# A fused attention and gated MLP block on one Trainium2 core: four tiles of x transposed once instead of twice, and the second half's preparation put on a fixed timetable

## The chip, the core and the metric

The kernel runs on one core of a Trainium2 chip. The metric is the device time of one execution in microseconds (us). The engines are TensorE (PE in the profile, with its weight loads as PEld), VectorE (DVE), ScalarE (ACT), GpSimd (POOL) and SyncE (SP), which here issues most of the DMAs. Each engine works through a queue of its own in order, and semaphores hold an instruction until its operands are there.

## The reference

```python
def reference(A_x, A_k_cache, A_v_cache, A_wq, A_wo, B_x, B_w_in, B_w_sp, B_b_sp, B_w_out):
    def _A_ref(x, k_cache, v_cache, wq, wo):      # 32 heads of 128, keys: the last 512
        q = (x @ wq).reshape(B, Sq, Hq, Dh).transpose(0, 2, 1, 3)
        k, v = k_cache[:, :, Sk - W:, :], v_cache[:, :, Sk - W:, :]
        scores = jnp.einsum("bhqd,bhkd->bhqk", q, k) * (Dh ** -0.5)
        o = jnp.einsum("bhqk,bhkd->bhqd", _softmax(scores), v)
        return o.transpose(0, 2, 1, 3).reshape(B, Sq, Hq * Dh) @ wo
    def _B_ref(x, w_in, w_sp, b_sp, w_out):
        z = _gelu(x @ w_in)
        z1, z2 = z[..., :Fh], _layernorm(z[..., Fh:])
        g = jnp.einsum("ts,bsf->btf", w_sp, z2) + b_sp[None, :, None]
        return (z1 * g) @ w_out
    xn = _layernorm(A_x)
    return A_x + _A_ref(xn, ...) * _silu(_B_ref(xn, ...))
```

x is 2048 rows of 512; Fh is 688. All is float32.

## The kernel before

Every float32 product is made of three TensorE matmuls: each operand is split into a high part (a rounded copy, made by ACT) and a low part (the rest, a subtraction on DVE or POOL), and `mm3` adds high by high, low by high and high by low. x is cut into 16 tiles of 128 rows, T8 = 8 in each half.

**The opening.** Tiles 0 to 7 are loaded into `sacc`, normalized (`ln_open` takes the statistics, `ln_apply` and `ln_apply_late` apply them) and transposed. `ln_flip(i)` makes four 128 by 128 transpositions against the unit matrix `ident` into one PSUM bank, ACT copies the high halves into the blocks `X`, and DVE subtracts for the low halves (`rest`). Tiles 4 to 7 have besides a copy of half the bank to `sacc` (L237) and one subtraction (L244), since q's projection is made with seven block products in place of eight (Strassen's scheme, Winograd's form): it needs sums T1 to T4 of quarters of x. Those pair tile p with tile p + 4. `t_sums(p)` transposes tile p a second time (line L215) and makes the sums in three subtractions and additions of 256 columns (L250 to L252); `t_split(p)` splits them. Between the transpositions stand pieces of z = x w_in (`z1_piece`, 12 matmuls of 344 columns), stored to DRAM by ACT's own DMA queue.

**The attention loop.** A step t makes for one tile of queries of one head the scores (`score`, lines L65 to L67 on `qT`), the maximum (`nm`, DVE's reduction at L530), the exponentials (ACT, L532), and for earlier steps the transposition of the probabilities (`turn`, DVE, L541, through DRAM: `p_dram`), their split (`shares`: ACT L560, POOL `pT_l`), the product with V (`pv`, L568 to L570), and the product with w_o (`outp`, L65 to L67 on `oT`), which DVE adds to `sacc` (L592). Four steps are a block; 16 steps are a round g of q's projection (`q_products`, L503, with `q_sum`, `q_split`, `q_evict`, `q_done`). I call s = (t + 12) mod 16 the phase of a step in its round. In a step, what the table `todo` holds comes before the score's reduction in DVE's, ACT's and POOL's order; the list `late` comes at the step's end, after `turn`.

**The second half of x.** The tiles 8 to 15 are prepared during the loop, in four passes p = 0 to 3 of `later_x(p)`, 48 steps (three rounds) apart. A pass loads two tiles (a and b), takes statistics (`tile_stats`), turns the variance into a factor (`row_stats`, with the small DVE operation at L74), applies it (ACT), transposes through DVE and DRAM (`turn_x`, `send`, `fetch`, `ordered`), and makes the quarter sums on POOL (`part`, and `sums(0)` to `sums(3)` at L356), which are stored to DRAM. Before, the rows of this sequence stood at t = max(t + 2, 30 + 12n // 5), every two or three steps: the statistics of a pass at t = 37 and 39, `row_stats` at 42, the two turns at 46 and 49, `part` at 63, the sums at 66, 68, 70 and 73 (for p = 0).

PSUM has eight banks in two pools of four. `ps_acc` holds q's products, `pv` and most z tiles, `ps_step` the scores, `outp` and, in the opening, the transpositions; both hand out their banks in turn. After the loop z's second half is made, tile by tile, each read by ACT's gelu (L846); the pools are then given up and the products with w_sp begin (L932) in the same banks.

Of the kernel before, what the change touches and what calls it, by code (L numbers as in the profile page):

```python
# [8 lines left out]
F32 = mybir.dt.float32  # L9
# [3 lines left out]
OP = mybir.AluOpType  # L13
# [27 lines left out]
def mixer_kernel(ctx: ExitStack, tc: tile.TileContext, x, wh, w_in, w_sp, b_sp, w_out, out):  # L41
# [8 lines left out]
    nc = tc.nc  # L50
# [10 lines left out]
    late = []  # L61
# [21 lines left out]
    ps_acc = psum.enter_context(tc.tile_pool(name="ps_acc", bufs=4, space=PSUM))  # L83
    ps_step = psum.enter_context(tc.tile_pool(name="ps_step", bufs=4, space=PSUM))
# [127 lines left out]
    def flip(t, late=False):  # L212
        ps = ps_acc.tile([P, NC, P], F32, name="ps_a") if late else ps_step.tile([P, NC, P], F32, name="ps_3")
        for c in range(NC):
            nc.tensor.transpose(ps[:, c, :], t[:, c * P:(c + 1) * P], ident)  # L215
        return ps

    def ln_flip(i, parts=1):
        n, j = divmod(i, 4)
        if j == 0:  # L220
            for h in range(2):
                X[0][h, n] = block()
        if parts == 1:
            ps = flip(sacc[:, i, :])
        else:
            ps = ps_step.tile([P, NC, P], F32, name="ps_3")
        rests, rest_of = [], []
        for h in range(2):
            if parts > 1:
                for c in (2 * h, 2 * h + 1):  # L230
                    nc.tensor.transpose(ps[:, c, :], sacc[:, i, c * P:(c + 1) * P], ident)
            hi, lo = (quarter(X[0][h, n][:, a], j) for a in range(2))
            nc.scalar.copy(hi, ps[:, 2 * h:2 * h + 2])
            rests.append((lo, ps[:, 2 * h:2 * h + 2], hi))
        if n == 1:
            p2, y = ps.rearrange("p c q -> p (c q)"), sacc[:, i, :]
            nc.scalar.copy(y[:, :256], p2[:, :256])  # L237
            rest_of.append((y[:, 256:], p2[:, 256:], y[:, :256]))
        if parts > 1:
            return rests  # L240
        for r in rests:
            rest(nc.vector, *r)
        for r in rest_of:
            nc.vector.tensor_tensor(*r, op=OP.subtract)  # L244

    TS = ("T2", "T1", "T3", "T4")

    def row_sums(ps, y, o):

        nc.vector.tensor_tensor(o[:, :256], y[:, :256], ps[:, :256], op=OP.subtract)  # L250
        nc.vector.tensor_tensor(o[:, 256:], ps[:, :256], y[:, 256:], op=OP.add)
        nc.vector.tensor_tensor(y[:, :256], ps[:, 256:], o[:, 256:], op=OP.subtract)  # L252

    def t_sums(p):
        if p == 0:
            X[0].update((k, block()) for k in TS)
        row_sums(flip(sacc[:, p, :]).rearrange("p c q -> p (c q)"), sacc[:, 4 + p, :], sacc[:, p, :])

    def t_split(p):
        y, o = sacc[:, 4 + p, :], sacc[:, p, :]  # L260
# [38 lines left out]
    def later_x(p):  # L299

        a, b, key = T8 + p, T8 + 4 + p, 100 * (p + 1)
        t, nb = {}, {}

        def row():
            return xq.tile([P, 512], F32, name="rawx")
# [52 lines left out]
        def store(*ks):  # L358
            for k in ks:
# [7 lines left out]
                                      t[k].bitcast(F32).rearrange("p (a c q) -> p a c q", a=2, q=P))  # L367

        seq = [load, None, None, lambda: tile_stats(t[a], key, 0), lambda: tile_stats(t[b], key, 1), row_stats,
               lambda: apply(b),  # L370
               lambda: (turn_x(b), apply(a)),
               lambda: turn_x(a),
               None,
               lambda: fetch(b),
# [33 lines left out]
    def z1_out(i, n, ps):  # L408
        z = zs.tile([P, NB], F32, name="z1")
        nc.scalar.copy(z, ps[:, :NB])  # L410
        nc.scalar.dma_start(z1_dram[:, i, n * NB:(n + 1) * NB], z)

    def z1_piece(i, n, between=lambda: None):
        z1_out(i, n, z1_product(i, n, between))
# [182 lines left out]
    T0, T1 = -QL, NSTEP + OL  # L597
# [3 lines left out]
    def at(t, f, *args):  # L601
        todo.setdefault(t, []).append((f, args))
# [52 lines left out]
                q_events.setdefault(t0 + done + 2, []).append((q_done, g, k))  # L655

    for p in range(4):
        at(-3 + p, t_sums, p)
        at(-2 + p, t_split, p)
    ends = {}  # L660
    ends.setdefault(-2, []).append((keep_x, (0, 1)))
# [7 lines left out]
    ends.setdefault(16 * (NG - 1) - LEAD + 9, []).append((fetch_x, 1, (0, 1)))  # L669
    for k in ((0, 0), (1, 0)):  # L670
        ends.setdefault(NSTEP + 6, []).append((fetch_x, 0, k))
    n, t = 0, 28
    for p in range(4):
        seq, store = later_x(p)
        for k, (f, ks) in enumerate(seq):
            t = max(t + 2, 30 + 12 * n // 5)
            for key in ks:
                at(t, store, key)
            if f:
                at(t, f)  # L680
            n += 1

    load_x(0, 1)
    load_early(0, [(0, 2)])
# [9 lines left out]
    ident = const.tile([P, P], F32, name="ident")  # L694
# [22 lines left out]
    ps = ps_step.tile([P, 512], F32, name="ps_3")  # L717
# [8 lines left out]
    ps = ps_step.tile([P, 512], F32, name="ps_3")  # L726
# [6 lines left out]
    ps = ps_acc.tile([P, 512], F32, name="ps_a")  # L733
# [8 lines left out]
    rest(nc.vector, *lowq)  # L742
    z1_out(0, 1, ps)
    z1_out(1, 1, ps1)
    ln_apply(rows[4], 4)
    ln_apply(rows[5], 5)
    z1_piece(2, 0)
    ln_open(6)
    ln_open(7)
    z1_piece(2, 1)  # L750

    FILL = dict(zip((-7, -6, -5, -4, -3, -2, -1, 0, 1, 8),
                    [(i, 1) for i in range(3, T8)] + [(i, 0) for i in range(4, T8)] + [(3, 0)]))
# [2 lines left out]
    for t in range(T0, T1):  # L756
# [6 lines left out]
        i = t + XL  # L763
# [21 lines left out]
        if t in DRAIN:  # L785
            ps = z1_product(*DRAIN[t])
# [21 lines left out]
    ps = z1_product(*LAST[-1])  # L808
# [422 lines left out]
```

## Time and profile before

| what | value |
|---|---|
| device time, median of 3 runs | 1761.42 us (1761.37 to 1762.11) |
| the profiled execution, its own time | 1761.58 us |
| its span, first to last instruction | 1759.7 us |
| busy: PE, PEld, DVE | 1753.1, 1503.3, 1489.9 us |
| busy: POOL, ACT | 1239.4, 1185.8 us |
| granted TensorE clock | 1.0 of full speed throughout |

The profiled execution's span leaves out what lies before the first and after the last instruction, 1.9 us here. A busy share says how long an engine had an instruction in hand. Matmuls overlap in the pipeline: one of 512 columns lasts 0.39 us in the rows, but the next one starts some 0.23 us after it, so short waits of PE don't show as idle time; they show in the distances between starts.

### The profile page before, as it was taken

To read this page: it belongs to the slowest core of one execution; us is meant where nothing else is said; L and a number is where in the kernel's file an instruction comes from. 1 tells how busy PE (TensorE), PEld (TensorE's weight loads), DVE (VectorE), ACT (ScalarE), POOL (GpSimd) and SP (SyncE) were. 2 spreads that over 40 slices of the span, in tenths; PEclk is the share of its full clock that TensorE was granted. 3 is DMA by queue.
4 is the path that set the end of the run, shared out by engine and by line. 5 is a ranking of instruction groups with operands and counts; after the bars stand their busy time and mean duration, and the time that the engine had idled before them with its cause. 6 is when DMAs were issued, how large, how long until landed. Compare 5 with 4: busy or idle time off the path is not lost.

```text
span 1759.7 us, 28541 instructions
## 1 busy us (share of the span) xinstructions
PE 1753.1 (100%) x8431; PEld 1503.3 (85%) x8431; DVE 1489.9 (85%) x2458; ACT 1185.8 (67%) x2621; POOL 1239.4 (70%) x1171
## 2 busy tenths in 40 slices
PE   9999999999999999999999999999999999999999
PEld 8888888888888887888888888888888899999997
DVE  6789889899899889988888888888888647887875
ACT  5877777777777777777777777777777546543333
POOL 2888998988988989888888888888888411000032
PEclk9999999999999999999999999999999999999999
DMA  6688888988989989788787777877888652655496
GB/s 204 213 237 260 260 250 242 261 240 244 269 246 253 258 235 273 223 255 223 223 228 219 232 225 220 226 218 225 229 224 255 210 192 86 223 189 176 149 259 204
DMA packets 177468, 398.45 MB, mean 226 GB/s; under 512 B 24480, under 2 KB 58528, under 8 KB 158112
## 3 DMA queue, kind: packets, MB, share of 16 engines
q1 hardware_dynamic: 172704, 390.99, 75.7%
q10 hardware_dynamic: 4608, 5.64, 0.9%
q8 instruction: 66, 1.08, 0.3%
q14 instruction: 90, 0.74, 0.1%
HBM read 231.65 MB, written 164.89 MB: 225 GB/s over the span
## 4 chain that ended last, share of the span: by engine, by line
PE 99%; ACT 0%; DVE 0%; issue 0%; POOL 0%; DVEq 0%; POOLq 0%; ACTq 0%
PE ps_a L503 17%; PE ps L65 13%; PE ps L67 13%; PE ps L66 13%; PE ps L932 11%; PE ps_a L570 7%; PE ps_a L569 7%; PE ps_a L568 7%; PE ps_a L66 2%; PE ps_a L67 2%; PE ps_a L65 2%; PE ps_f L66 1%; PE ps_f L67 1%; PE ps_f L65 1%; PE ps_f L932 1%; PE ps_f L1139 0%
## 5 line engine op out<-in xcount | busy, mean ns | idle before, releaser
L59 POOL TENSOR_TENSOR pT_l<-pL,pT_h 128x512 fp32r<-128x512 f32 x507 | 659.2, 1303 | 170.9 <-ACT pT_h L560 162.6
L532 ACT ACTIVATE prob<-ps,nm 128x512 f32<-128x512 f32 x512 | 353.6, 691 | 340.8 <-DVE nm L530 331.8
L592 DVE SCALAR_TENSOR_TENSOR sacc<-ps,sums,sacc 128x512 f32<-128x512 f32 x496 | 369.3, 745 | 115.0 <-PE ps L67 109.4
L503 PE MATMUL ps_a<-x,x 128*128 128x512 f32 x1266 | 365.5, 389 | 0.0
L541 DVE STREAM_TRANSPOSE pL<-prob 128x512 f32<-128x512 f32 x512 | 358.6, 700 | 0.4 <-ACT prob L532 0.4
L530 DVE TENSOR_REDUCE nm<-ps 128x1 f32<-128x512 f32 x512 | 339.9, 664 | 3.0 <-PE ps L67 2.9
L560 ACT CAST pT_h<-pL 128x512 fp32r<-128x512 f32 x512 | 318.5, 622 | 7.3 <-ACT z L410 4.9
L503 PEld LDWEIGHTS ps_a<-x,x 128*128 128x128 f32 x1266 | 237.7, 188 | 49.3 <-issue 0.2
L59 POOL TENSOR_TENSOR wl<-raw,wh 128x512 fp32r<-128x512 f32 x186 | 241.9, 1300 | 11.0 <-ACT wh L145 11.0
L65 PE MATMUL ps<-wh,qT_h 128*128 128x512 f32 x512 | 200.7, 392 | 0.3 <-DVE sacc L592 0.2
L67 PE MATMUL ps<-wh,qT_l 128*128 128x512 f32 x512 | 200.0, 391 | 0.0
L570 PE MATMUL ps_a<-pT_l,wh 128*128 128x512 f32 x512 | 199.6, 390 | 0.0
L65 PE MATMUL ps<-wh,oT_h 128*128 128x512 f32 x512 | 199.4, 390 | 0.0
L66 PE MATMUL ps<-wl,qT_h 128*128 128x512 f32 x512 | 199.4, 389 | 0.0
L66 PE MATMUL ps<-wl,oT_h 128*128 128x512 f32 x512 | 199.4, 389 | 0.0
L568 PE MATMUL ps_a<-pT_h,wh 128*128 128x512 f32 x512 | 199.4, 389 | 0.0
L569 PE MATMUL ps_a<-pT_h,wl 128*128 128x512 f32 x512 | 199.4, 389 | 0.0
L67 PE MATMUL ps<-wh,oT_l 128*128 128x512 f32 x512 | 199.3, 389 | 0.0
L932 PE MATMUL ps<-b,x 128*128 128x344 f32 x1248 | 191.8, 316 | 0.0
L932 PEld LDWEIGHTS ps<-b,x 128*128 128x128 f32 x1248 | 191.5, 188 | 0.0
L59 POOL TENSOR_TENSOR b<-b 128x512 fp32r<-128x512 f32 x2 | 2.5, 1293 | 189.5 <-DMA x<-x 189.5
L59 POOL TENSOR_TENSOR x<-wq,x 128x256 fp32r<-128x256 f32 x177 | 131.6, 744 | 0.0
(212 smaller groups left out, 3047.7 us busy)
## 6 DMA issues: line engine op xcount, KB each, us to landing
p_dram<-pL SPq DMA_DIRECT2D x128, 1024.0 KB, 4.8
pL<-p_dram SPq DMA_DIRECT2D x256, 192.0 KB, 4.1
raw<-wh SPq DMA_DIRECT2D x188, 256.0 KB, 6.3
pL<-p_dram SPq DMA_DIRECT2D x256, 128.0 KB, 4.1
x<-w_sp SPq DMA_DIRECT2D x24, 1024.0 KB, 5.1
pL<-p_dram SPq DMA_DIRECT2D x256, 64.0 KB, 4.0
wq<-wh SPq DMA_DIRECT2D x60, 256.0 KB, 5.7
z_dram<-z ACTq DMA_DIRECT2D x32, 172.0 KB, 3.0
```

Source lines behind the costliest of these rows:

```text
L59: engine.tensor_tensor(lo, whole, hi.bitcast(F32), op=OP.subtract)
L65: nc.tensor.matmul(ps, lh, rh, start=first, stop=False)
L66: nc.tensor.matmul(ps, lh, rl, start=False, stop=False)
L67: nc.tensor.matmul(ps, ll, rh, start=False, stop=last)
L503: nc.tensor.matmul(qps[g, bank], wt["q", g, k][a][:, c * P:(c + 1) * P], X[g * 2 // H][ORDER[k]][:, b, c], start=first, stop=r == 5, skip_ ...
L530: nc.vector.tensor_reduce(nm, ps, axis=AX.X, op=OP.max, negate=True)
L532: nc.scalar.activation(prob[t], ps, AF.Exp, bias=nm, accum_out=sums[b][:, j:j + 1])
L541: nc.vector.transpose(pL[b][:, :, j * P:j * P + P].rearrange("p a (c q) -> p a c q", q=Q), prob.pop(t).rearrange("p (a c q) -> p a c q", a ...
L568: nc.tensor.matmul(pps[b], vh, ph, start=c == 0, stop=False)
L570: nc.tensor.matmul(pps[b], vh, pl, start=False, stop=c == 3)
L592: nc.vector.scalar_tensor_tensor(at, ps, rs, at, op0=OP.mult, op1=OP.add)
L932: nc.tensor.matmul(ps, a, b, start=k != "P4" and c == 0 and m == 0, stop=c == RP - 1 and m == 2, skip_group_check=True)
```

## The change

Three things change. First, tiles 0 to 3 are transposed once: ACT copies the whole bank of each transposition to SBUF (`keep_whole`, four copies of 128 by 512 between the z pieces of the opening; the first two transpositions go to `ps_acc` for that), and the sums are made from this copy at the end of the steps in which tiles 4 to 7 are transposed, in four subtractions (`row_sums`, after the other work of the step, in `late`). `t_sums` with its transpositions is gone; `t_blocks` only sets up the blocks. Second, one transposition of the unit matrix stands ahead of the last z tile, which moves that tile to the next bank. Third, the passes of `later_x` have a table of steps, 28 + 48 p plus 4, 14, 17 and so on, and the two applications stand together in one step.

```diff
+    def keep_whole(i):
+        p2, whole[i] = whole[i], xq.tile([P, 512], F32, name="rawx")
+        nc.scalar.copy(whole[i], p2)
...
         if parts == 1:
-            ps = flip(sacc[:, i, :])
+            ps = flip(sacc[:, i, :], i == 1)
         else:
-            ps = ps_step.tile([P, NC, P], F32, name="ps_3")
-        rests, rest_of = [], []
+            ps = ps_acc.tile([P, NC, P], F32, name="ps_a")
+        rests = []
...
+        p2 = ps.rearrange("p c q -> p (c q)")
         if n == 1:
-            p2, y = ps.rearrange("p c q -> p (c q)"), sacc[:, i, :]
+            y = sacc[:, i, :]
             nc.scalar.copy(y[:, :256], p2[:, :256])
-            rest_of.append((y[:, 256:], p2[:, 256:], y[:, :256]))
+            late.append((row_sums, p2, y, sacc[:, i - 4, :], whole[i - 4]))
+        whole[i] = p2
...
-    def row_sums(ps, y, o):
-
-        nc.vector.tensor_tensor(o[:, :256], y[:, :256], ps[:, :256], op=OP.subtract)
-        nc.vector.tensor_tensor(o[:, 256:], ps[:, :256], y[:, 256:], op=OP.add)
-        nc.vector.tensor_tensor(y[:, :256], ps[:, 256:], o[:, 256:], op=OP.subtract)
-
-    def t_sums(p):
-        if p == 0:
-            X[0].update((k, block()) for k in TS)
-        row_sums(flip(sacc[:, p, :]).rearrange("p c q -> p (c q)"), sacc[:, 4 + p, :], sacc[:, p, :])
+    def row_sums(ps, y, o, x):
+
+        for to, x0, x1 in ((y[:, 256:], ps[:, 256:], y[:, :256]), (o[:, :256], ps[:, :256], x[:, :256]),
+                           (o[:, 256:], ps[:, 256:], o[:, :256]), (y[:, :256], x[:, 256:], o[:, 256:])):
+            nc.vector.tensor_tensor(to, x0, x1, op=OP.subtract)
...
-               lambda: apply(b),
-               lambda: (turn_x(b), apply(a)),
+               lambda: (apply(b), apply(a)),
+               lambda: turn_x(b),
...
+    STORE_X = {"b": 32, "a": 33, (1, 1): 45, (0, 0): 46, (1, 0): 46, (0, 1): 48, "T1": 48, "T3": 49, "T2": 50, "T4": 51}
+    WHEN_X = (4, 0, 0, 14, 17, 18, 20, 30, 31, 0, 38, 39, 43, 44, 46, 47, 48, 49, 50)
...
-            t = max(t + 2, 30 + 12 * n // 5)
+            t = 28 + 48 * p + (WHEN_X[k] if k < len(WHEN_X) else 0)
...
+    keep_whole(0)
     ln_apply(rows[4], 4)
     ln_apply(rows[5], 5)
-    z1_piece(2, 0)
+    z1_piece(2, 0, lambda: keep_whole(1))
     ln_open(6)
     ln_open(7)
-    z1_piece(2, 1)
+    z1_piece(2, 1, lambda: (keep_whole(2), keep_whole(3)))
...
+            if (pos, n) == (NT - 1, 3):
+                nc.tensor.transpose(ps_acc.tile([P, 512], F32, name="ps_a")[:, :P], ident, ident)
```

Three places show what moves. On PE, at step -3 of the opening (the end of q's first projection, `x_185` by the query weights `wh_325`, and the start of the z piece of tile 7), before:

```order
L65 MATMUL ps_a<-x_185,wh_325 128x512
L66 MATMUL ps_a<-x_185,wh_325 128x512
L67 MATMUL ps_a<-x_185,wl_326 128x512
L215 MATMUL ps_542<-ident,sacc 128x128 x4
L65 MATMUL ps_a<-wh_245,x_405 128x344
L66 MATMUL ps_a<-wl_246,x_405 128x344
L67 MATMUL ps_a<-wh_245,x_405 128x344
```

and now, on the same engine at the same place:

```order
L65 MATMUL ps_a<-x_185,wh_325 128x512
L66 MATMUL ps_a<-x_185,wh_325 128x512
L67 MATMUL ps_a<-x_185,wl_326 128x512
L65 MATMUL ps_a<-wh_245,x_413 128x344
L66 MATMUL ps_a<-wl_246,x_413 128x344
L67 MATMUL ps_a<-wh_245,x_413 128x344
```

The row of four transpositions is gone; it goes likewise at steps -2, -1 and 0, and nothing else of PE's order changes but the one transposition ahead of the last z tile.

On DVE, at steps -7 and -6 of the opening (the low halves of tiles 4 and 5, and the application of the statistics to tiles 6 and 7), before:

```order
L59 TENSOR_TENSOR x_405<-ps_407,x_405 128x2x128
L59 TENSOR_TENSOR x_406<-ps_407,x_406 128x2x128
L244 TENSOR_TENSOR sacc<-ps_407,sacc 128x256
L200 SCALAR_TENSOR_TENSOR sacc<-sacc,mv,rs_r 128x512
L59 TENSOR_TENSOR x_405<-ps_439,x_405 128x2x128
L59 TENSOR_TENSOR x_406<-ps_439,x_406 128x2x128
L244 TENSOR_TENSOR sacc<-ps_439,sacc 128x256
L200 SCALAR_TENSOR_TENSOR sacc<-sacc,mv,rs_r 128x512
```

and now (`rawx` is ACT's copy of the earlier tile, in SBUF):

```order
L59 TENSOR_TENSOR x_413<-ps_415,x_413 128x2x128
L59 TENSOR_TENSOR x_414<-ps_415,x_414 128x2x128
L200 SCALAR_TENSOR_TENSOR sacc<-sacc,mv,rs_r 128x512
L258 TENSOR_TENSOR sacc<-ps_415,sacc 128x256
L258 TENSOR_TENSOR sacc<-ps_415,rawx 128x256
L258 TENSOR_TENSOR sacc<-ps_415,sacc 128x256
L258 TENSOR_TENSOR sacc<-rawx,sacc 128x256
L59 TENSOR_TENSOR x_413<-ps_450,x_413 128x2x128
L59 TENSOR_TENSOR x_414<-ps_450,x_414 128x2x128
L200 SCALAR_TENSOR_TENSOR sacc<-sacc,mv,rs_r 128x512
```

Four subtractions stand now between two tiles where one stood; the three that are added came from the steps -3 to 0, and the last of the four reads SBUF alone.

On POOL, in the phases 7 to 11 of a round (`x_770` and `x_758` are split query weights, `wl` the low half of a weight piece), before, in a round that held none of the sums:

```order
L59 TENSOR_TENSOR wl_3076<-raw,wh_3075 128x512
L59 TENSOR_TENSOR x_770<-wq,x_770 128x256
L59 TENSOR_TENSOR pT_l<-pL,pT_h 128x512
L59 TENSOR_TENSOR wl_3108<-raw,wh_3107 128x512
L59 TENSOR_TENSOR pT_l<-pL,pT_h 128x512 x2
L59 TENSOR_TENSOR wl_3175<-raw,wh_3174 128x512
L59 TENSOR_TENSOR x_770<-wq,x_770 128x256
L59 TENSOR_TENSOR pT_l<-pL,pT_h 128x512
```

and now, in the round that ends a pass:

```order
L59 TENSOR_TENSOR wl_3054<-raw,wh_3053 128x512
L59 TENSOR_TENSOR x_758<-wq,x_758 128x256
L360 TENSOR_TENSOR rawx<-rawx 128x256
L59 TENSOR_TENSOR pT_l<-pL,pT_h 128x512
L59 TENSOR_TENSOR wl_3088<-raw,wh_3087 128x512
L360 TENSOR_TENSOR rawx<-rawx 128x256
L59 TENSOR_TENSOR pT_l<-pL,pT_h 128x512
L360 TENSOR_TENSOR rawx<-rawx 128x256
L59 TENSOR_TENSOR pT_l<-pL,pT_h 128x512
L59 TENSOR_TENSOR wl_3160<-raw,wh_3159 128x512
L59 TENSOR_TENSOR x_758<-wq,x_758 128x256
L360 TENSOR_TENSOR rawx<-rawx 128x256
```

The four sums stand now in four steps one after the other, with `part` (a row `rawx<-rawx` at L59) just ahead of them; before, they were spread over the phases 11 to 5 of the next round.

## Rows read from the trace of the kernel before

**Rows 1.** The page, part 1: busy time, share of the span, instructions.

```profile
PE 1753.1 (100%) x8431; PEld 1503.3 (85%) x8431; DVE 1489.9 (85%) x2458; ACT 1185.8 (67%) x2621; POOL 1239.4 (70%) x1171
```

**Rows 2.** Timeline of PE: first score matmul of steps 36, 68, 84, 228 (start, duration).

```profile
126.04 0.39 PE L65 MATMUL ps<-wh,qT_h 128*128 128x512 f32 x1
...
210.96 0.39 PE L65 MATMUL ps<-wh,qT_h 128*128 128x512 f32 x1
...
253.12 0.39 PE L65 MATMUL ps<-wh,qT_h 128*128 128x512 f32 x1
...
634.33 0.39 PE L65 MATMUL ps<-wh,qT_h 128*128 128x512 f32 x1
```

**Rows 3.** Timeline of three engines around step 42, phase 6.

```profile
144.53 1.29 POOL L59 TENSOR_TENSOR pT_l<-pL,pT_h 128x512 fp32r<-128x512 f32 x1 [1.98 <-ACT pT_h L560]
...
144.58 1.27 DVE L74 TENSOR_SCALAR rs_t<-mv 128x2 f32<-128x2 f32 x1
...
146.36 0.73 DVE L592 SCALAR_TENSOR_TENSOR sacc<-ps,sums,sacc 128x512 f32<-128x512 f32 x1
...
147.15 0.49 PE L65 MATMUL ps<-wh,qT_h 128*128 128x512 f32 x1
```

**Rows 4.** Timeline of DVE and PE around step 51, phase 15.

```profile
165.74 0.67 DVE L801 STREAM_TRANSPOSE rawx<-rawx 128x512 f32<-128x512 f32 x1
...
168.37 0.69 DVE L59 TENSOR_TENSOR qT_l<-ps_a,qT_h 128x512 fp32r<-128x512 f32 x1
...
169.12 0.50 PE L67 MATMUL ps<-wh,qT_l 128*128 128x512 f32 x1
```

**Rows 5.** The chain that ended last, 33 to 43 us: start, length, piece.

```profile
33.30 0.44 PE ps L215 x4
...
42.38 0.44 PE ps L215 x4
```

**Rows 6.** Timeline of ACT, DVE, PE and POOL in the opening.

```profile
20.67 0.45 ACT L410 COPY z<-ps 128x344 f32<-128x344 f32 x1 [1.08 <-DMA z_dram<-z]
...
22.95 0.39 ACT L237 COPY sacc<-ps 128x256 f32<-128x256 f32 x1
...
23.37 0.75 DVE L59 TENSOR_TENSOR x<-ps,x 128x256 fp32r<-128x256 f32 x2 [0.59 <-ACT sacc L237]
...
24.81 0.32 PE L67 MATMUL ps_a<-wh,x 128*128 128x344 f32 x1
...
29.23 1.29 POOL L59 TENSOR_TENSOR wl<-raw,wh 128x512 fp32r<-128x512 f32 x1 [5.68 <-ACT wh L145]
```

**Rows 7.** Timeline of POOL and DVE around step 255.

```profile
707.70 1.29 POOL L59 TENSOR_TENSOR wl<-raw,wh 128x512 fp32r<-128x512 f32 x1
...
707.86 1.68 DVE L59 TENSOR_TENSOR x<-x 128x512 fp32r<-128x512 f32 x1
```

**Rows 8.** Timeline of DVE and PE: statistics at step 37; step 106 without a pass.

```profile
130.66 0.68 DVE L177 BATCH_NORM_STATS2 stt<-rawx 128x6 f32<-128x512 f32 x1
...
131.47 0.66 DVE L530 TENSOR_REDUCE nm<-ps 128x1 f32<-128x512 f32 x1
...
315.02 0.74 DVE L592 SCALAR_TENSOR_TENSOR sacc<-ps,sums,sacc 128x512 f32<-128x512 f32 x1
...
316.96 0.39 PE L65 MATMUL ps<-wh,qT_h 128*128 128x512 f32 x1
```

**Rows 9.** Timeline of POOL and PE, steps 107 to 111, in a round without sums.

```profile
317.04 1.30 POOL L59 TENSOR_TENSOR pT_l<-pL,pT_h 128x512 fp32r<-128x512 f32 x1 [0.68 <-ACT pT_h L560]
...
319.56 0.73 POOL L59 TENSOR_TENSOR x<-wq,x 128x256 fp32r<-128x256 f32 x1
...
331.69 0.39 PE L570 MATMUL ps_a<-pT_l,wh 128*128 128x512 f32 x1
```

**Rows 10.** Timeline of ACT and PE at the end of z.

```profile
1490.63 0.80 ACT L846 ACTIVATE b<-ps_a 128x344 f32<-128x344 f32 x2
...
1487.24 0.93 PE L932 MATMUL ps<-b,x 128*128 128x344 f32 x5
```

More of the change, by code (lines that the diff above doesn't have):

```diff
@@ L216, in flip @@
         return ps
+    whole = {}
+    def keep_whole(i):
+        p2, whole[i] = whole[i], xq.tile([P, 512], F32, name="rawx")
+        nc.scalar.copy(whole[i], p2)
     def ln_flip(i, parts=1):
@@ L242, in ln_flip, with t_blocks @@
             rest(nc.vector, *r)
-        for r in rest_of:
-            nc.vector.tensor_tensor(*r, op=OP.subtract)
     TS = ("T2", "T1", "T3", "T4")
-    def row_sums(ps, y, o):
-        nc.vector.tensor_tensor(o[:, :256], y[:, :256], ps[:, :256], op=OP.subtract)
-        nc.vector.tensor_tensor(o[:, 256:], ps[:, :256], y[:, 256:], op=OP.add)
-        nc.vector.tensor_tensor(y[:, :256], ps[:, 256:], o[:, 256:], op=OP.subtract)
-    def t_sums(p):
-        if p == 0:
-            X[0].update((k, block()) for k in TS)
-        row_sums(flip(sacc[:, p, :]).rearrange("p c q -> p (c q)"), sacc[:, 4 + p, :], sacc[:, p, :])
+    def row_sums(ps, y, o, x):
+        for to, x0, x1 in ((y[:, 256:], ps[:, 256:], y[:, :256]), (o[:, :256], ps[:, :256], x[:, :256]),
+                           (o[:, 256:], ps[:, 256:], o[:, :256]), (y[:, :256], x[:, 256:], o[:, 256:])):
+            nc.vector.tensor_tensor(to, x0, x1, op=OP.subtract)
+    def t_blocks():
+        X[0].update((k, block()) for k in TS)
     def t_split(p):
@@ L657, in mixer_kernel @@
     for p in range(4):
-        at(-3 + p, t_sums, p)
+        if p == 0:
+            at(-3, t_blocks)
         at(-2 + p, t_split, p)
@@ L671, in mixer_kernel @@
         ends.setdefault(NSTEP + 6, []).append((fetch_x, 0, k))
-    n, t = 0, 28
+    STORE_X = {"b": 32, "a": 33, (1, 1): 45, (0, 0): 46, (1, 0): 46, (0, 1): 48, "T1": 48, "T3": 49, "T2": 50, "T4": 51}
+    WHEN_X = (4, 0, 0, 14, 17, 18, 20, 30, 31, 0, 38, 39, 43, 44, 46, 47, 48, 49, 50)
     for p in range(4):
@@ L675, in mixer_kernel @@
         for k, (f, ks) in enumerate(seq):
-            t = max(t + 2, 30 + 12 * n // 5)
+            t = 28 + 48 * p + (WHEN_X[k] if k < len(WHEN_X) else 0)
             for key in ks:
-                at(t, store, key)
+                at(28 + 48 * p + STORE_X[key], store, key)
             if f:
                 at(t, f)
-            n += 1
     load_x(0, 1)
```

## The prediction

> **What bounds the kernel now.** I read the page first, then the distances between TensorE's starts. TensorE is busy throughout [rows 1], so the time changes only where it gets fewer instructions or where a short wait goes or comes, and such a wait shows as a start that is late. The timeline of the score matmuls gives the measure: two rounds' first scores, at 210.96 and 253.12, lie 42.16 us apart with no pass of later_x between them that costs anything [rows 2]. From step 36 to step 228 there are twelve rounds and four passes: 634.33 - 126.04 = 508.29 us, against 12 x 42.16 = 505.92. So the four passes cost **2.37 us**, 0.59 each [rows 2].
>
> The timelines around a pass show two places. At step 42 the small DVE operation of `row_stats` starts 0.05 us after a POOL `pT_l`, lasts 1.27 us for two columns and ends when POOL ends; the eviction of w_o's product behind it in DVE's queue ends at 146.36 + 0.73 = 147.09, its bank comes free too late, and the score matmul at 147.15 lasts 0.49 instead of 0.39 [rows 3]. At step 51 the transposition of `turn_x` at 165.74 stands ahead of `qT_l` in DVE's queue; `qT_l` ends at 169.06, and the score matmul that reads it, at 169.12, waits and lasts 0.50 [rows 4]. Neither shows as idle time of PE.
>
> **The change, part by part.** *Transpositions of steps -3 to 0.* The chain gives each group of four 0.44 us [rows 5], on PE, which has nothing else to do meanwhile: 4 x 0.44 = **-1.76**. Nothing takes their place on PE.
>
> *Passes on a timetable.* Relative to its round a pass now always has the same phases: statistics at 6 and 9, `row_stats` at 10, both applications at 12, turns at 6 and 7 of the next round, `part` and the sums at 6 to 10 of the round after. If these places are free, all of the 2.37 goes: **-2.37**. For DVE the tightest is phase 6. Statistics put 131.47 - 130.66 = 0.81 us ahead of the next work [rows 8]. In a round without a pass the eviction there starts at 315.02; with 0.81 more it would end at 315.02 + 0.74 + 0.81 = 316.57, and the next score starts at 316.96: 0.39 us are left [rows 8]. A turn takes 0.67 and stands at the same place [rows 4]; it no longer stands in the phases 13 to 15, ahead of a `qT_l`. The small operation at phase 10 can again be held for 1.27; if an eviction is late there too, that gives back some 0.1 us in each pass, the excess of [rows 3], 0.4 in all. I take nothing, since it needs both a POOL start just ahead and a tight bank.
>
> For POOL the sums are now five operations in five steps one after the other. In order, from the `pT_l` at 317.04 to that of step 111, POOL's queue holds seven operations of 512 columns and, with the four sums, six of 256. The former last 1.30 and the latter 0.73 in the rows [rows 9]; back to back the next one starts a little before the end, and I take 1.25 and 0.70 from start to start, so the last `pT_l` starts at 317.04 + 8.75 + 4.20 = 329.99 and ends near 331.28. The matmul that reads it starts at 331.69 [rows 9]: 0.4 us are left, and I take nothing for it. What was 3 us of cover is then almost used up; if POOL were later, `pv` waits, and everything behind it on PE.
>
> *The transposition of the unit matrix.* One instead of four: between 0.44 / 4 = 0.11 and 0.44 [rows 5]; nothing has to be waited for, so the near end, **+0.12**. What it buys: the banks of `ps_acc` go in turn, and without it the last z tile's bank would, by the removal of other tiles, be that of the first product with w_sp. That product starts at 1487.24, while the last gelu ends at 1490.63 + 0.80 = 1491.43 [rows 10]: a wait of 4.2 us, if the bank were the same.
>
> *ACT in the opening.* Four copies of 128 by 512 from PSUM are new. No row shows one; one of 256 columns takes 0.39 [rows 6], so one takes 0.39 to 0.78. I take 0.51, as 344 columns take 0.45 [rows 6] and the time grows less than the width: 2.04 in all. ACT waits there for its own z stores, 1.08 before 20.67 [rows 6], and part of this is cover: I take three quarters, 0.81, and leave the rest to the issue of the stores. ACT is then 1.23 late. Its copy at 22.95 would end at 23.34 + 1.23 = 24.57, and DVE, which begins the low halves of tile 4 when that copy is done (23.37 follows 23.34), begins at 24.6 instead; its first half is there near 25.0. The z piece's third matmul reads it; it started at 24.81 and its weights are loaded some 0.16 (a matmul's pitch there) ahead [rows 6]. So PE waits about 0.25 and 0.1 for the restart: **+0.35**. Bounds: nothing if ACT's waits cover it all, 1.4 if none of it (0.81 more on top of 0.35, and the longer copies).
>
> *DVE in the opening.* Per tile DVE now has two low halves (0.67), an application (0.66), and four subtractions (1.55, 256 columns each, near 0.39 a piece as ACT's copy [rows 6]): 2.9 us, against (42.38 - 33.30) / 3 = 3.03 for a step [rows 5]. It keeps up, but regains little. The fourth subtraction reads SBUF with both operands. Tile 5's would start at 24.6 + 2 x 2.9 - 0.4 = 30.0, while POOL's `wl` runs from 29.23 [rows 6], with the 0.35 from 29.6 to 30.9. The trace has such a meeting: a DVE operation with two SBUF operands that started at 707.86, 0.16 after POOL's, took 1.68 and ended 0.55 after it [rows 7]; one of half the width would end some 0.3 after, at 31.2. The low half of tile 6 is then there near 31.5, and needed at 24.81 + 2 x 3.03 + 0.35 - 0.16 = 31.06: 0.45 late, with the restart **+0.55**; bounds 0 and 0.7.
>
> The Trainium skill ("SBUF — State Buffer", section "Who interferes with whom") says that a DVE instruction with two SBUF inputs contends with a GpSimd instruction that reads SBUF, and that whichever issues second is blocked fully. By that rule the subtraction is blocked and the sum has the 0.55; without it the sum would be 0.55 lower. The trace agrees, by the 1.68 us.
>
> *Sum.* -1.76 - 2.37 + 0.12 + 0.35 + 0.55 = -3.11. The profiled execution took 1761.58, so 1758.47; it lies 0.16 above the median of the runs, 1761.42, so **1758.3**.
>
> **The rivals.**
> *The opening waits for nothing, or for less.* For it: both waits rest on a copy whose length no row shows, and on meetings of some tenths. Against it: DVE already waits for ACT's copy (0.59 us before 23.37 [rows 6]), so any delay of ACT there is passed on. With the first wait alone 1757.8, with none 1757.4.
> *Sums moderately late.* POOL has 0.4 us to spare in each of four rounds, 3% of the 13 us that I counted. A loss of 0.1 to 0.7 per round gives 1758.9 to 1761.
> *Statistics too tight at phase 6.* Another 0.1 to 0.5 per pass, when the first of the two statistics or a turn meets a late eviction (0.39 us to spare [rows 8]): 1758.6 to 1760.5.
> *Slower than before: POOL behind by whole operations.* The five operations, 5 x 0.70 = 3.5 us, come one after the other in phases in which POOL also makes `pT_l` in every step. If the DVE reading of two SBUF operands holds POOL too, as [rows 7] shows it held DVE, each round loses what exceeds the 0.4. It decides at 3.11 / 4 = 0.78 us lost per round; one more POOL operation of 1.3 in the window [rows 9] would do, at 1761.4 + 4 x (0.9 - 0.78) = 1762. Slower by 0.2% needs 1.66 per round: (3.11 + 3.52) / 4. Against it: idle time stands ahead of 317.04, 0.68 us [rows 9], so POOL isn't behind when the window opens.
> *The bank isn't the one meant.* If the last z tile shares its bank with the first product with w_sp, that waits 4.2 us [rows 10]: 1762.5.
>
> **How the numbers follow.** 0.2% is 3.52 us, about what a measurement of this kernel can tell from no change: faster means below 1757.9, slower above 1764.9. Chances: my forecast, 1758.3 with its own range of 1757.9 to 1759.0, 0.40; opening waits smaller or none, 0.25; sums moderately late, 0.18; statistics too tight, 0.07; POOL behind by whole operations, 0.07; the bank, 0.03. The predicted time is that of the first. Faster takes the second case whole and the lower edge of the first, 0.34; slower takes most of the fifth, 0.06; the rest, 0.60, is within. A range from 1757.0 (a little under no waits at all) to 1760.8 leaves out the upper end of three cases and the last, under 0.2.
>
> **What would show it.** Right: no transpositions at 33 to 43 us; rounds of 42.16 throughout steps 36 to 228, so that this stretch takes 505.9 and not 508.3; in the opening a lengthened third matmul in tile 4's z piece and again in tile 6's, with a subtraction of over 1 us on DVE near 30 us beside POOL's `wl`; the four copies of ACT near 0.5 each; POOL's last `pT_l` of the window some 0.4 us ahead of its matmul; the first product with w_sp without a wait. Wrong: scores or `pv` matmuls late in the phases 7 to 12 of a pass's rounds, a longer copy, or an ACT delay that goes on past the tiles 4 to 7 into the first exponentials. The prediction would fail most if POOL's queue in the sums' rounds were longer than counted, since each pass repeats it four times.

## The result and the profile after

The changed kernel is slower: 1767.93 us (median of 6 runs, 1767.42 to 1768.35) against 1761.76 us, a ratio of 1.0035 with a 95% interval of 1.0022 to 1.0048. The prediction was 1758.3 us, with a range from 1757.0 to 1760.8. Each measured time of a kernel is the median of its undisturbed executions; one of 5583 us, in the run with the fourth subtraction on POOL, is left out.

The page, part 1 of the kernel after, has fifteen matmuls fewer than [rows 1] and 5.9 us more of busy PE, so the matmuls that are left take longer:

```profile
PE 1759.0 (100%) x8416; PEld 1507.6 (85%) x8416; DVE 1486.9 (84%) x2458; ACT 1187.9 (67%) x2625; POOL 1238.6 (70%) x1171
```

The same starts as in [rows 2], of steps 36 and 228, in the kernel after:

```profile
125.39 0.39 PE L65 MATMUL ps<-wh,qT_h 128*128 128x512 f32 x1
...
634.68 0.39 PE L65 MATMUL ps<-wh,qT_h 128*128 128x512 f32 x1
```

The profiled execution (1768.14 us, span 1765.9) is 6.56 us longer than that of before. Up to step 36 it gained 0.65 (126.04 to 125.39). The four passes, from step 36 to 228, take 509.29 in place of 508.29: 1.00 lost, where 2.37 were to be gained. From step 228 to step 504, near the end of the loop, the two differ by 0.05. From there to the end of the span it is 5.89 longer, and 0.36 lies outside the span. So nearly the whole loss is behind the loop. PE around the transposition of the unit matrix (L1002), and two later stretches of the products with w_sp (start, duration, count):

```profile
1483.86 0.32 PE L65 MATMUL ps_a<-wh,x 128*128 128x344 f32 x1
...
1485.55 0.32 PE L67 MATMUL ps_a<-wh,x 128*128 128x344 f32 x1
1485.70 0.27 PE L1002 MATMUL ps_a<-ident 128*128 128x128 f32 x1
1485.73 0.40 PE L65 MATMUL ps_a<-wh,x 128*128 128x344 f32 x1
1485.97 0.32 PE L66 MATMUL ps_a<-wl,x 128*128 128x344 f32 x1
...
1487.55 0.32 PE L67 MATMUL ps_a<-raw,x 128*128 128x344 f32 x1
1487.71 0.48 PE L938 MATMUL ps<-b,x 128*128 128x344 f32 x2
...
1499.70 10.57 PE L938 MATMUL ps<-b,x 128*128 128x344 f32 x66
```

I call the distance from one start to the next the pitch. Ahead of the transposition eleven pitches lie between 1483.86 and 1485.55, 1.69 / 11 = 0.154 us each; behind it ten lie between 1485.97 and 1487.55, 0.158 each, and 12 us later it is still so: (10.57 - 0.32) / 65 = 0.1577 us. The kernel before kept 0.153 there: five of these products take 0.93 in [rows 10], (0.93 - 0.32) / 4. Between 1490 and 1700 us the mean distance between starts of neighbouring 344-column matmuls is 153.33 ns before and 157.77 ns after; 4.44 ns for each of the some 1340 such distances behind the transposition are 5.9 us. The clock isn't it, since the granted clock is 1.0 in both. The first product with w_sp starts at 1487.71 without a wait, while the last gelu runs until 1491.73 in the trace, so the bank was moved as intended.

In the passes, the loss is at step 52. POOL, ACT, DVE and PE there, after:

```profile
155.01 1.30 POOL L59 TENSOR_TENSOR pT_l<-pL,pT_h 128x512 fp32r<-128x512 f32 x1 [0.67 <-ACT pT_h L564]
156.28 1.29 POOL L59 TENSOR_TENSOR wl<-raw,wh 128x512 fp32r<-128x512 f32 x1
...
158.24 0.70 POOL L75 TENSOR_TENSOR rs_r<-rs_t,power 128x2 f32<-128x2 f32 x1
158.99 0.65 DVE L534 TENSOR_REDUCE nm<-ps 128x1 f32<-128x512 f32 x1
159.03 0.50 POOL L321 TENSOR_SCALAR rs_t<-mv,rs_r 128x1 f32<-128x1 f32 x2
159.57 1.52 ACT L324 ACTIVATE rawx<-rawx,rs_t,rs_r 128x512 f32<-128x512 f32 x2 [1.34 <-POOL rs_t L321]
161.00 0.67 ACT L536 ACTIVATE prob<-ps,nm 128x512 f32<-128x512 f32 x1
...
162.78 0.69 DVE L59 TENSOR_TENSOR oT_l<-ps_a,oT_h 128x512 fp32r<-128x512 f32 x1 [1.53 <-ACT oT_h L582]
...
166.61 0.69 ACT L536 ACTIVATE prob<-ps,nm 128x512 f32<-128x512 f32 x1 [1.16 <-DVE nm L534]
...
167.28 0.58 ACT L437 CAST qT_h<-ps_a 128x512 fp32r<-128x512 f32 x1
...
167.40 0.39 PE L67 MATMUL ps<-wh,oT_l 128*128 128x512 f32 x1
167.92 0.50 PE L65 MATMUL ps<-wh,qT_h 128*128 128x512 f32 x1
```

This is read from top to bottom. `row_stats` stands in POOL's queue behind `pT_l`, `wl` and a split of query weights, so the factor is there only at 159.5. ACT has been idle for 1.34 us by then and starts both applications at 159.57; the exponential behind them, whose maximum was ready at 159.64, starts at 161.00. `oT_h` is late, DVE is idle for 1.53 us waiting for it, and DVE's queue stays late from there on. At step 51 the exponential waits 1.16 for its maximum, `qT_h` behind it ends at 167.86, and the score matmul of step 52 starts at 167.92, 0.52 after the one ahead of it, where 0.23 is usual. Set against the run further down in which the applications are moved, this start is 0.37 us late (167.92 - 125.39 against 166.76 - 124.60), and by the start of step 53 its trace and this one differ by 0.77: the other 0.40 lies within step 52, whose third score matmul reads `qT_l`.

The kernel before lost the same 0.40 in this step, at the third score matmul [rows 4], and another 0.2 at step 42 [rows 3]. At step 52 the trace points to `turn_x`: it stood ahead of the maximum in DVE's queue, so ACT's exponential came late, and `qT_h` (167.76 to 168.34) behind it, for which `qT_l` waited until 168.37 (before):

```profile
167.08 0.69 ACT L532 ACTIVATE prob<-ps,nm 128x512 f32<-128x512 f32 x1 [1.75 <-DVE nm L530]
```

So the change took one cause of a late exponential away and put another in its place. That `turn_x` was the first is read from this trace; no run moves it alone.

### The profile page after: what moved, and what is told of

Same layout as the page of the kernel before. It is cut to its first block, busy times and chain, and to the rows that moved or that the text cites. A ratio compares the mean times of both kernels' runs of the same rounds, so it can differ in the third digit from the quotient of the medians.

```text
span 1765.9 us, 28509 instructions
## 1 busy us (share of the span) xinstructions
PE 1759.0 (100%) x8416; PEld 1507.6 (85%) x8416; DVE 1486.9 (84%) x2458; ACT 1187.9 (67%) x2625; POOL 1238.6 (70%) x1171
## 4 chain that ended last, share of the span: by engine, by line
PE 98%; DMA 0%; DVE 0%; ACT 0%; issue 0%; POOL 0%; ACTq 0%; DVEq 0%; POOLq 0%
PE ps_a L507 17%; PE ps L65 13%; PE ps L67 13%; PE ps L66 13%; PE ps L938 11%; PE ps_a L573 6%; PE ps_a L572 6%; PE ps_a L574 6%; PE ps_a L67 2%; PE ps_a L65 2%; PE ps_a L66 2%; PE ps_f L67 1%; PE ps_f L65 1%; PE ps_f L66 1%; PE ps_f L938 1%; PE ps_f L1147 0%
## 5 line engine op out<-in xcount | busy, mean ns | idle before, releaser
L59 POOL TENSOR_TENSOR pT_l<-pL,pT_h 128x512 fp32r<-128x512 f32 x507 | 658.1, 1301 | 173.6 <-ACT pT_h L564 162.2
L59 POOL TENSOR_TENSOR wl<-raw,wh 128x512 fp32r<-128x512 f32 x186 | 241.7, 1299 | 9.7 <-DVE sacc L258 5.8
L65 PE MATMUL ps<-wh,qT_h 128*128 128x512 f32 x512 | 200.3, 391 | 0.8
L67 PE MATMUL ps<-wh,qT_l 128*128 128x512 f32 x512 | 199.8, 390 | 0.0
L65 PE MATMUL ps<-wh,oT_h 128*128 128x512 f32 x512 | 199.3, 389 | 0.0
L66 PE MATMUL ps<-wl,qT_h 128*128 128x512 f32 x512 | 199.3, 389 | 0.0
L67 PE MATMUL ps<-wh,oT_l 128*128 128x512 f32 x512 | 199.2, 389 | 0.0
L66 PE MATMUL ps<-wl,oT_h 128*128 128x512 f32 x512 | 199.2, 389 | 0.0
L938 PE MATMUL ps<-b,x 128*128 128x344 f32 x1248 | 197.4, 319 | 0.0
L938 PEld LDWEIGHTS ps<-b,x 128*128 128x128 f32 x1248 | 197.0, 188 | 0.0
L59 POOL TENSOR_TENSOR b<-b 128x512 fp32r<-128x512 f32 x2 | 2.6, 1298 | 195.2 <-ACT b L1108 195.2
L59 POOL TENSOR_TENSOR x<-wq,x 128x256 fp32r<-128x256 f32 x177 | 131.3, 742 | 0.0
```

Source lines behind the costliest of these rows:

```text
L59: engine.tensor_tensor(lo, whole, hi.bitcast(F32), op=OP.subtract)
L65: nc.tensor.matmul(ps, lh, rh, start=first, stop=False)
L66: nc.tensor.matmul(ps, lh, rl, start=False, stop=False)
L67: nc.tensor.matmul(ps, ll, rh, start=False, stop=last)
L938: nc.tensor.matmul(ps, a, b, start=k != "P4" and c == 0 and m == 0, stop=c == RP - 1 and m == 2, skip_group_check=True)
```

## The experiments

**Without the transposition.**

```diff
-            if (pos, n) == (NT - 1, 3):
-                nc.tensor.transpose(ps_acc.tile([P, 512], F32, name="ps_a")[:, :P], ident, ident)
```

> The changed kernel without the transposition of the unit matrix ahead of the last z tile. In the changed kernel the matmuls of 344 columns start every 153.3 ns up to that transposition and every 157.8 ns from it to the end, 4.4 ns more for each of some 1330 matmuls, 5.9 us. Theory (rhythm: the transposition throws TensorE into a slower rhythm that then keeps): without it the pitch stays at 153.3 ns, but the last z tile shares its bank with the first product with w_sp, which waits about 4 us for the last gelu: 1767.9 - 5.9 - 0.2 + 4.0 = 1765.8 us, if the wait itself does not set the slow rhythm, 1771.7 if it does. Rival (the order of banks that the change leaves costs the 4.4 ns): the pitch stays at 157.8 and the wait comes on top, 1771.7 us.

Measured: 1774.16 us, ratio to before 1.007 (1.0055 to 1.0085). PE, and the granted clock (PEclk) in two stretches (us, PE busy, PEclk, DMA share, GB/s):

```profile
1487.77 0.31 PE L67 MATMUL ps_a<-raw,x 128*128 128x344 f32 x1
1492.19 4.49 PE L938 MATMUL ps<-b,x 128*128 128x344 f32 x17 [4.10 <-ACT b L852]
...
1499.83 10.42 PE L938 MATMUL ps<-b,x 128*128 128x344 f32 x65
```

```profile
1492.40:1495.40 3.00, 3.00 (x12) 0.53 0.00 0
1496.40:1500.00 3.60, 3.60 (x25) 1.00 0.21 33
```

The bank is shared, as expected: the product waits 4.42 us from the last start, for the gelu. Two things come on top. The granted clock after this wait is 0.53 over some 3 us, the 1.2 GHz level for most of it: twelve matmuls start 0.28 to 0.29 us apart in place of 0.158, which costs 1.5 us. And the pitch behind it is (10.42 - 0.32) / 64 = 0.158 us: after the wait and the fall of the clock the slow pitch is there too, with no short matmul. So this run can't tell the theory from its rival. The expectation named that case, at 1771.7, but without the clock.

**A matmul as wide as its neighbours.**

```diff
-                nc.tensor.transpose(ps_acc.tile([P, 512], F32, name="ps_a")[:, :P], ident, ident)
+                nc.tensor.matmul(ps_acc.tile([P, 512], F32, name="ps_a")[:, :NB], x_op(i, 0, 0), wt[("w", n), 0][0][:, :NB],
+                                 start=True, stop=True)
```

> The changed kernel with a plain matmul of 344 columns, whose result nobody reads, in place of the transposition of the unit matrix: the bank moves as in the changed kernel. Rhythm: the pitch stays at 153.3 ns to the end, 1767.9 - 5.9 = 1762.0 us. Rival (bank order): 157.8 ns, 1767.9 us.

Measured: 1761.65 us, ratio 0.9999 (0.9990 to 1.0009). PE:

```profile
1485.45 0.32 PE L1002 MATMUL ps_a<-wh,x 128*128 128x344 f32 x1
...
1499.71 9.98 PE L938 MATMUL ps<-b,x 128*128 128x344 f32 x64
```

The pitch stays: (9.98 - 0.32) / 63 = 0.153. The same banks, 6.3 us less than the changed kernel: the order of banks isn't the cause.

**A matmul of 128 columns, no transposition.**

```diff
-                nc.tensor.transpose(ps_acc.tile([P, 512], F32, name="ps_a")[:, :P], ident, ident)
+                nc.tensor.matmul(ps_acc.tile([P, 512], F32, name="ps_a")[:, :P], x_op(i, 0, 0), wt[("w", n), 0][0][:, :P],
+                                 start=True, stop=True)
```

> The changed kernel with a plain matmul of 128 columns in place of the transposition of the unit matrix. If it is the length (a matmul shorter than the load of the next weights behind it) that throws TensorE into the slow rhythm: 157.8 ns from there and 1767.9 us. If it is what a float32 transposition does, and not its length: 153.3 ns and 1762.0 us. Bank order: 1767.9 us.

Measured: 1767.87 us, ratio 1.0035 (1.0022 to 1.0048), as the changed kernel. PE:

```profile
1485.59 0.22 PE L1002 MATMUL ps_a<-wh,x 128*128 128x128 f32 x1
1485.65 0.37 PE L65 MATMUL ps_a<-wh,x 128*128 128x344 f32 x1
...
1499.74 10.58 PE L938 MATMUL ps<-b,x 128*128 128x344 f32 x66
```

0.158 again. It is the short matmul, not what a float32 transposition does: the next matmul starts 0.06 later.

**The kernel before with one transposition, no bank moved.**

```diff
+        if (i, n) == (ZO[-1], 3):
+            nc.tensor.transpose(zps[i, n][:, :P], ident, ident)
         zmm(zps[i, n][:, :NB], i, n, range(NC))
```

> The kernel before with one transposition of the unit matrix into the bank of the last z tile, ahead of that tile's first matmul, which overwrites it: no bank moves. Rhythm: 157.8 ns from there on, 1761.7 + 0.2 + 5.8 = 1767.7 us. Rival (bank order): 153.3 ns, 1761.9 us.

Measured: 1767.75 us, ratio 1.0034 (1.0021 to 1.0048). PE, 14 us behind the transposition:

```profile
1499.83 10.42 PE L934 MATMUL ps<-b,x 128*128 128x344 f32 x65
```

The pitch is (10.42 - 0.32) / 64 = 0.158 us; between 1489 and 1700 us its mean is 157.78 ns. That one instruction alone costs the kernel before 6 us.

**What ends the rhythm.**

```diff
+                turned = ps_acc.tile([P, 512], F32, name="ps_a")
+                nc.tensor.transpose(turned[:, :P], ident, ident)
+                for k in range(12):
+                    nc.tensor.matmul(turned, x_op(i, 0, 0), X[i // T8][0, i % T8 // 4][:, 0, 0, :], start=True, stop=True)
```

> The changed kernel with twelve matmuls of 512 columns, whose results nobody reads, behind the transposition of the unit matrix. In the loop, whose matmuls have 512 columns, the pitch after a stall is irregular (228 to 236 ns) for some eight matmuls and then 226.7 again. Theory: a matmul longer than the load of the next weights lets TensorE's weight loads catch up, so the twelve end the slow rhythm: 153.3 ns behind them, and 1767.9 - 5.8 + 12 x 0.23 = 1764.9 us. Rival (the rhythm of the 344-column matmuls does not depend on what ran before them, or the twelve leave it as it is): 157.8 ns and 1770.7 us.

Measured: 1764.27 us, ratio 1.0015 (1.0005 to 1.0024). PE, the products with w_sp:

```profile
1499.69 10.59 PE L938 MATMUL ps<-b,x 128*128 128x344 f32 x68
```

(10.59 - 0.32) / 67 = 0.153: the twelve wider matmuls ended the slow pitch, at 0.23 us each, and that was still cheaper than to keep it. That 512 columns leave the loads time to catch up was the reason given for it; the run shows that the rhythm ends, not why.

**The applications later.**

```diff
-    WHEN_X = (4, 0, 0, 14, 17, 18, 20, 30, 31, 0, 38, 39, 43, 44, 46, 47, 48, 49, 50)
+    WHEN_X = (4, 0, 0, 14, 17, 18, 25, 30, 31, 0, 38, 39, 43, 44, 46, 47, 48, 49, 50)
```

> The changed kernel with the two applications of a pass five steps later (25 in place of 20 in the table of steps, phase 1 in place of 12). In the changed kernel ACT waits 1.34 us for POOL's rs_t ahead of the applications at 159.57 us, its exponentials, oT_h and qT_h come late, and the score matmul of step 52 starts some 0.3 us late; from step 36 to 228 the four passes lose 3.4 us against rounds of 42.16. Theory (the applications stand too close behind row_stats): nearly all of the 3.4 goes, 1764.5 us, and steps 36 to 228 take 506.0. Rival (DVE's or POOL's queue sets the loss): 509.3 and 1767.9 us.

Measured: 1764.72 us, ratio 1.0016 (1.0007 to 1.0025). Steps 36, 52 and 228:

```profile
124.60 0.39 PE L65 MATMUL ps<-wh,qT_h 128*128 128x512 f32 x1
...
166.76 0.39 PE L65 MATMUL ps<-wh,qT_h 128*128 128x512 f32 x1
...
630.61 0.39 PE L65 MATMUL ps<-wh,qT_h 128*128 128x512 f32 x1
```

630.61 - 124.60 = 506.01: the passes cost 0.09 us now, all four together (12 x 42.16 = 505.92), and the score of step 52 is undelayed (0.39). So the other places of the table, on DVE and POOL, were as good as free.

**The fourth subtraction on POOL.**

```diff
-                           (o[:, 256:], ps[:, 256:], o[:, :256]), (y[:, :256], x[:, 256:], o[:, 256:])):
+                           (o[:, 256:], ps[:, 256:], o[:, :256])):
             nc.vector.tensor_tensor(to, x0, x1, op=OP.subtract)
+        nc.gpsimd.tensor_tensor(y[:, :256], x[:, 256:], o[:, 256:], op=OP.subtract)
```

> The changed kernel with the fourth of the four subtractions of a tile, the one that reads SBUF with both operands, on POOL in place of DVE. Theory (DVE's two-operand subtraction at 30.40 us is held 0.7 us by POOL's wl, and the third matmul of tile 6's z piece waits 0.33 and restarts in 0.1): that wait goes, 1767.5 us, and the stretch from the first matmul of 17.8 us to step 0 is 0.4 us shorter. Rival: POOL's wl now waits behind the subtraction, which waits for DVE, and q's next product waits for wl instead: 1767.9 or later.

Measured: 1767.51 us (median of five, 1767.35 to 1767.83), ratio 1.0032 (1.002 to 1.0044), which the times alone don't tell from the changed kernel. First the changed kernel, DVE's subtractions of tiles 4 and 5 that read SBUF alone, POOL's `wl`, and the third matmul of tile 6's z piece:

```profile
27.49 0.42 DVE L258 TENSOR_TENSOR sacc<-rawx,sacc 128x256 f32<-128x256 f32 x1
...
29.94 1.29 POOL L59 TENSOR_TENSOR wl<-raw,wh 128x512 fp32r<-128x512 f32 x1 [5.76 <-DVE sacc L258]
30.40 1.11 DVE L258 TENSOR_TENSOR sacc<-rawx,sacc 128x256 f32<-128x256 f32 x1
...
31.41 0.32 PE L66 MATMUL ps_a<-wl,x 128*128 128x344 f32 x1
31.90 0.42 PE L67 MATMUL ps_a<-wh,x 128*128 128x344 f32 x1 [0.17 <-DVE x L59]
32.16 0.31 PE L65 MATMUL ps_a<-wh,x 128*128 128x344 f32 x1
```

and with the fourth subtraction on POOL:

```profile
29.85 0.74 POOL L259 TENSOR_TENSOR sacc<-rawx,sacc 128x256 f32<-128x256 f32 x1 [1.90 <-PE ps_a L67]
30.55 1.30 POOL L59 TENSOR_TENSOR wl<-raw,wh 128x512 fp32r<-128x512 f32 x1
...
30.96 0.31 PE L66 MATMUL ps_a<-wl,x 128*128 128x344 f32 x1
...
31.27 0.32 PE L65 MATMUL ps_a<-wh,x 128*128 128x344 f32 x1
```

From L66 to the next L65 it is 0.75 us in the one and 0.31 in the other: 0.44 less. The subtraction that began 0.46 after POOL's `wl` lasted 1.11 in place of 0.42. `wl` now comes 0.6 later, and no matmul of the opening waits for it: from 17 us to step 0 no two starts lie more than 0.25 us apart.

**All three.** The matmul of 344 columns, the applications at 25 and the fourth subtraction on POOL, each edit as above.

> The changed kernel with the plain matmul of 344 columns in place of the transposition of the unit matrix, the applications five steps later and the fourth subtraction on POOL. If the three losses are separate: 1767.9 - 6.2 - 3.4 - 0.4 = 1757.9 us. If one of them only hides another: between 1758.3 and 1761.7 us.

Measured: 1758.08 us, ratio 0.9979 (0.9970 to 0.9987): faster than both kernels, and near the 1757.9 of the sum. The two large losses are separate; that the 0.4 of the third comes on top is less than these times can show, and rests on the trace, in which no two starts of the opening from 17 us to step 0 lie more than 0.25 us apart. Step 36 stands at 124.49 and step 228 at 630.50 in its trace, 506.01 apart, and the pitch behind the loop is 153.33 ns.

**The factor earlier, the applications in their place.**

```diff
-    WHEN_X = (4, 0, 0, 14, 17, 18, 20, 30, 31, 0, 38, 39, 43, 44, 46, 47, 48, 49, 50)
+    WHEN_X = (4, 0, 0, 14, 17, 17, 20, 30, 31, 0, 38, 39, 43, 44, 46, 47, 48, 49, 50)
```

> The changed kernel with row_stats in the step of the second statistics (17 in place of 18 in the table of steps), the applications where they are. In the changed kernel the two applications of the first pass start at 159.57 us, when rs_t is there, last 1.52, and the exponential behind them, whose maximum was there at 159.64, starts at 161.00; ACT was idle for 1.34 us ahead of them. Theory (rs_t comes late, as POOL makes it behind three other operations): with rs_t there 1.3 us or more earlier the applications run in that idle time, the exponential is not late, and of the 3.4 us of the four passes nearly all goes: 1764.5 us. Rival (two applications in a row at phase 12 are too much for ACT wherever their factor comes): 1767.9 us, or little less.

Measured: 1766.10 us, ratio 1.0026 (1.0016 to 1.0036), between the two. Steps 36 to 228 take 507.84. DVE in step 45 and PE's scores of steps 47 and 52:

```profile
151.14 0.68 DVE L177 BATCH_NORM_STATS2 stt<-rawx 128x6 f32<-128x512 f32 x1
...
152.07 0.59 DVE L74 TENSOR_SCALAR rs_t<-mv 128x2 f32<-128x2 f32 x1
...
153.18 0.74 DVE L596 SCALAR_TENSOR_TENSOR sacc<-ps,sums,sacc 128x512 f32<-128x512 f32 x1
...
153.97 0.50 PE L65 MATMUL ps<-wh,qT_h 128*128 128x512 f32 x1
...
167.52 0.39 PE L65 MATMUL ps<-wh,qT_h 128*128 128x512 f32 x1
```

The late score of step 52 is gone (0.39): with the factor there in time the two applications in a row don't delay it, so the rival falls. But the statistics and the small operation of `row_stats`, held 0.59, now stand in one step of DVE, the eviction ends at 153.92, and the score of step 47 starts at 153.97 and is late instead.

**One application later.**

```diff
-               lambda: (apply(b), apply(a)),
+               lambda: apply(b),
...
-    WHEN_X = (4, 0, 0, 14, 17, 18, 20, 30, 31, 0, 38, 39, 43, 44, 46, 47, 48, 49, 50)
+    WHEN_X = (4, 0, 0, 14, 17, 18, 20, 30, 31, 25, 38, 39, 43, 44, 46, 47, 48, 49, 50)
```

(the entry of 25 is `apply(a)`)

> The changed kernel with one of the two applications left at phase 12 behind row_stats and the other five steps later. The exponential would come 0.7 us late instead of 1.4. If the lateness of the exponential passes on to qT_h by its size: score of step 52 late by nothing or by 0.1, as some 0.5 to 0.7 us of it are absorbed on the way, 1765 us; if any application that waits for rs_t at that place costs the same: 1767.9 us.

Measured: 1765.06 us, ratio 1.0019 (1.001 to 1.0029); steps 36 to 228 take 506.51. Counted from step 36, the first late exponential starts 0.7 us earlier than in the changed kernel. Against the run above with both applications moved, the four passes cost 0.5 us in place of 3.3 (506.51 and 509.29, less 506.01): half the lateness is nearly all absorbed on the way, the whole of it is not.

## Why the prediction was wrong

**The transposition of the unit matrix: mis-sized, and by far the most.** The step was: "One instead of four: between 0.44 / 4 = 0.11 and 0.44 [rows 5]; nothing has to be waited for, so the near end, +0.12." The matmul itself is about that: from the start of the L67 ahead of it (1485.55) to that of the L66 behind the next matmul (1485.97), 0.42 us pass where two pitches would be 0.31. But the term priced the instruction by its own time and took the time of its neighbours as given. It cost 6 us, shown from three sides: put into the kernel before it costs 6.0 (1767.75 against 1761.7), replaced by a matmul of the neighbours' width it gives 6.3 back (1761.65), and followed by twelve wider ones the kernel is 2.6 slower than that (1764.27), about the 12 x 0.23 of the twelve. Why the short matmul does this stays open. What it bought was real: without it the wait was 4.42, where 4.2 stood in the prediction.

The trace of before held a hint. Its opening's z pieces stand behind transpositions, and nine distances lie between the matmul at 24.81 in [rows 6] and this one:

```profile
26.23 0.32 PE L67 MATMUL ps_a<-oT_h,x 128*128 128x344 f32 x1
```

That is 1.42 / 9 = 0.158, and the products behind the loop have 0.153 [rows 10]. The prediction used the first number, "some 0.16 (a matmul's pitch there)", without asking why it was not the other; the row that it points at shows no pitch.

**The passes: the step "If these places are free, all of the 2.37 goes" failed.** DVE's and POOL's places were checked and were as good as free: 506.01 with the applications moved. POOL's last `pT_l` of the sums, for one, ended 0.37 us ahead of its matmul in the first pass of the kernel after, where 0.4 was forecast:

```profile
244.61 1.31 POOL L59 TENSOR_TENSOR pT_l<-pL,pT_h 128x512 fp32r<-128x512 f32 x1
...
246.29 0.39 PE L574 MATMUL ps_a<-pT_l,wh 128*128 128x512 f32 x1
```

ACT's place was not checked. The applications at phase 12 were listed and not costed: neither what they wait for, POOL's part of `row_stats` two steps ahead of them, nor what stands behind them in ACT's queue. The trace of before already had this path: its `qT_l` was late through ACT's exponential, and the prediction put that down to DVE's queue alone. So one wait takes the place of the one removed; it costs (509.29 - 505.92) / 4 = 0.84 us per pass, against 0.59 before. The rival of this kind that was named, statistics too tight at phase 6, did not come.

**The opening: right in its mechanism, the first wait too large.** -1.76 for the transpositions and two waits were forecast, a net of -0.86 with 0.35 and 0.55. The trace has 0.08 for the first wait (0.23 from L67 to L65 below, where the pitch is 0.158) and 0.43 for the second, with DVE's two-operand subtraction held to 1.11 us by POOL's `wl`, as the sentence on [rows 7] said. ACT's copies take 1.07 for two, against 0.51 each:

```profile
20.31 1.07 ACT L222 COPY rawx<-ps_a 128x512 f32<-128x512 f32 x2 [0.40 <-ACT z L414]
...
25.43 0.39 PE L67 MATMUL ps_a<-wh,x 128*128 128x344 f32 x1
25.66 0.33 PE L65 MATMUL ps_a<-wh,x 128*128 128x344 f32 x1
```

The profiled execution gained only 0.54 by step 0. In it the statistics of the second tile of x, which wait for its load, start 0.56 us later than before (6.52 against 5.96), which takes about as much away. Step 0 stands at 42.03 in it and at 41.01 to 42.01 in seven other traces with the same opening, against 42.57 and 42.53 in two with the opening of before: one trace gives the gain of the opening to about a microsecond only.

The Trainium skill ("SBUF — State Buffer", section "Who interferes with whom"), by whose rule the prediction had the second wait, agrees with these traces: 1.11 us beside POOL's `wl` against 0.42 alone, and no such wait with the subtraction taken off DVE. With the two wrong terms put right the sum comes near: the three edits together, one of which also takes the second opening wait away, gave 1758.08 us. That this is close to the 1758.3 of the prediction is no support for it, since it is another kernel.

Two of the prediction's rivals have ends that its own steps don't give: 4 x 0.1 on top of 1758.3 is 1758.7, not 1758.9 or 1758.6, and 4 x 0.5 gives 1760.3, not 1760.5. Nothing hangs on it.

## What to carry to other kernels

On an engine that is always busy, an instruction has to be priced by what starts after it, too: in a stream of equal matmuls compare the pitch ahead of and behind an odd one. If a matmul is needed only to move a bank, make it as wide as its neighbours: here that took 6.3 us off. When work is put on a timetable, check every engine that the sequence passes through, in each place what the operation waits for and what is queued behind it; an in-order queue turns a wait for a factor nobody is in a hurry for into a late exponential. And a term that repeats four times or 1300 times deserves the first look.

## What was not expected of the hardware

In these traces TensorE keeps one of two rhythms in a stream of 344-column matmuls with a weight load each: 153.3 ns, all alike, or a mean of 157.8 ns, in a repeating series of 159, 156 and 158 to 159, at the same granted clock of 1.0. A matmul of 128 columns set the slow one, and so did a wait of 4.4 us with the fall of the clock behind it; it then lasted for over 1300 matmuls; twelve matmuls of 512 columns ended it. The kernel before fits this: slow in the opening, behind transpositions, and fast behind the loop, whose matmuls have 512 columns. In the loop a late start is followed by two to ten irregular distances (224 to 240 ns) and then 226.7 again, without help. The Trainium skill ("TensorE: Matmul & The Clock Gate", section "Back-to-back issue gap") says that in a stream of loads and matmuls the spacing is set by both. No run here separates the two shares, and what differs between the rhythms stays open: the weight loads last 188 ns each in both. Only 128, 344 and 512 columns were tried.

After the wait of 4.4 us, with TensorE idle, the granted clock was 0.53 over 3 us, the lower of its two levels (1.2 GHz) for most of them, and 1.0 again from 1496.4 us.
